# Hash products of the late head pairs ahead of the gated parts, q·k ahead of the bucket product, and another order of the first steps

## Chip, cores, metric

One core of a Trainium2 chip. The metric is device microseconds of one execution. Each comparison has its own runs of the kernel before on the same chip. A ratio is the mean time of one kernel's fast runs over that of the other's of the same rounds, so it is not quite the ratio of the medians quoted beside it.

## The reference, cut

```python
# attention, 4 batches x 8 heads x 768 x 64, 6 hash bits
q_bucket = sum((q @ proj > 0) * 2**i);  k_bucket = sum((k @ proj > 0) * 2**i)
scores = where(q_bucket == k_bucket, (q @ k.T) / 8, -1e9)
x = softmax(scores) @ v            # rearranged to 3072 x 512
# feed-forward
g = x @ w_gate;  out = (g * sigmoid(g) * (x @ w_val)) @ w_out
```

## The kernel before

Heads are worked in pairs, 16 pairs, numbered from 0 here ("pair 10" is the number). A pair has 12 score units (2 halves of queries x 6 chunks of keys), two to a step of the loop; I call these two scores a *duo* of scores, and the change from other matmuls to a duo a *turn*. A wait "in pair 10" is one for the signs of pair 10, while the scores of pair 9 run. A step issues in this order: two scores, the products with v of the step before, then parts ("atoms") of the feed-forward of the batch before, with pieces of the next pair's preparation between them. The schedule is manual: what is written first is first in each engine's order.

A *tile* is a buffer of the program; a *bank* is what its `bank` helper takes, 128 x 512 f32 of PSUM, and a score tile is declared as two of them. The late hash products land in such a tile, and *evictions* turn them into sign bits: the keys' on VectorE, the queries' on ScalarE. A *row* is one matmul record of the trace; an f32 product of one head is two rows (768 for 384 products), and the rows of the two heads run side by side (four take 0.81 us, at 486 ns each).

A score adds two products in PSUM: a bf16 product of sign bits, which is 0 for the same bucket and hugely negative otherwise, and the f32 product of q and k.

```python
sc_ps = tile_pool(name="sc_ps", bufs=2)      # tiles of two banks
mm_ps = tile_pool(name="mm_ps", bufs=3)      # tiles of one bank: parts of the feed-forward

def score(u):
    sc = score_tile("sc")
    for x, start in ((bits, True), (T, False)):          # bucket product, then q.k
        for h in range(2):
            nc.tensor.matmul(sc[:, h, 0:HQ], x["k", n][rows, ks], x["q", n][rows, qs], ...)
    nc.scalar.activation(ring[...], sc[:, :, 0:HQ], AF.Exp, scale=SCALE)

def hash_blocks():                            # pairs 8 to 15
    ps = front_bank("hps")                    # there: one bank of a two-bank score tile
    for i, (name, half) in enumerate(where):  # k0, k1, q0, q1: 32 rows each
        nc.tensor.matmul(ps[i*32 : (i+1)*32, 0:HQ], hash_w[name][:, 0:32], T[name, n][...])
    def evict(half, to):                      # keys' signs on VectorE, queries' on ScalarE
        ...
    return [four evictions, each of one key and one query block]

# the step
while atoms and credit >= atoms[0][0]:
    size, atom = atoms.pop(0)
    atom()                                    # a part: products, then its VectorE and ScalarE work
    while mine and size:                      # behind it: hash_blocks, later one eviction a part
        size -= 1
        mine[:1] = mine[0]() or []
```

The softmax here doesn't subtract the row's maximum and nothing guards it: scores larger than these inputs give would overflow.

Of the kernel before, what the change touches and what calls it, by code (L numbers as in the profile page):

```python
# [17 lines left out]
def kernel(  # L18
# [11 lines left out]
    nc = tc.nc  # L30
# [6 lines left out]
    HQ = CH * P  # L37
    BLOCK = 32
    NP = H // 2
# [30 lines left out]
    def bank(name):  # L70
        return mm_ps.tile([P, 512], FP32, tag="mm", name=name)

    def score_tile(name):
        return sc_ps.tile([P, 2, 512], FP32, tag="sc", name=name)
# [5 lines left out]
    def fetch(n, name, queue, half=None):  # L80
        b, pr = pairs[n]
        if name == "v":
            t = raws["v", n] = raw.tile([P, 2, NCH, D], FP32, tag="vraw", name="vraw")
            queue.dma_start(
                t.rearrange("p h c d -> p h (c d)"),
                v[b, 2 * pr : 2 * pr + 2].rearrange("h (p c) d -> p h (c d)", c=NCH),
            )
            return
        src = q if name == "q" else k
        if not half:  # L90
            raws[name, n] = raw.tile([P, NCH, 2, D], FP32, tag=name + "raw", name=name + "raw",
                                     bufs=1)
        t = raws[name, n]
        if n <= NP:
            cs = slice(None) if half is None else slice(half * CH, (half + 1) * CH)
            for h in range(2):
                queue.dma_start(t[:, cs, h, :],
                                src[b, 2 * pr + h].rearrange("(p c) d -> p c d", c=NCH)[:, cs, :])
            return


        blocks = t.rearrange("p c a b -> p (c a b)").rearrange(
            "p (c a d) -> p c a d", a=P // BLOCK, d=BLOCK)
        for h in range(2):
            for x in range(D // BLOCK):
                at = h * D + x * BLOCK
                queue.dma_start(
                    blocks[at : at + BLOCK],
                    src[b, 2 * pr + h][:, x * BLOCK : (x + 1) * BLOCK].rearrange(
                        "(a p c) d -> p c a d", c=NCH, p=BLOCK))  # L110

    def load(n):
        for name in "qkv":
            fetch(n, name, nc.sync)
# [20 lines left out]
    for _ in range(9):  # L135
        ps = bank("idle")
# [26 lines left out]
    hash_w = {}  # L163
# [36 lines left out]
    def load_words(i, queue=nc.gpsimd):  # L200
        if i < len(pieces):
            words[i] = wraw.tile([P, PIECE, 2], I32, tag="words", name="words")
            queue.dma_start(words[i].rearrange("p f w -> p (f w)"), pieces[i][1])
# [29 lines left out]
    def narrow_on(n):  # L233
        for _ in range(n):
            next(narrowing, None)

    load_words(0, nc.sync)
    load_words(1, nc.sync)
    load(1)


    T = {}
    bits = {}
    atoms = []

    def front_bank(name):

        if len(T) > 2 * 2 * NP:
            return score_tile(name)[:, 0, :]
        return bank(name)  # L250

    def front(n):


        def transpose(name, half):
            if (name, n) not in T:
                T[name, n] = opnd.tile([P, S], FP32, tag=name + "T", name=name + "T")
            ps = front_bank("tps")
            for i in range(CH):
                nc.tensor.transpose(ps[:, i * P : (i + 1) * P],  # L260
                                    raws[name, n][:, half * CH + i, :, :].rearrange("p h d -> p (h d)"),
                                    ident)
            nc.scalar.copy(T[name, n][:, half * HQ : (half + 1) * HQ], ps[:, 0:HQ])

        bits["q", n] = sides["q", n % 2]
        bits["k", n] = sides["k", n % 2]

        def sign(name, half, to, ps, at):
            o = bits[name, n][to, half * HQ : (half + 1) * HQ]
            if name == "q":  # L270
                nc.scalar.activation(o, ps[at, 0:HQ], AF.Sign, bias=nudge[to])  # L271
            else:
                nc.vector.tensor_scalar(o, ps[at, 0:HQ], scalar1=above_k[to], scalar2=times_k[to],  # L273
                                        op0=ALU.is_gt, op1=ALU.mult)

        def hash_bits(name, half):
            ps = front_bank("hps")
            nc.tensor.matmul(ps[:, 0:HQ], hash_w[name], T[name, n][:, half * HQ : (half + 1) * HQ],  # L278
                             start=True, stop=True)
            sign(name, half, slice(0, P), ps, slice(0, P))  # L280

        def hash_blocks():

            ps = front_bank("hps")
            where = [(name, half) for name in "kq" for half in range(2)]
            for i, (name, half) in enumerate(where):
                nc.tensor.matmul(ps[i * BLOCK : (i + 1) * BLOCK, 0:HQ], hash_w[name][:, 0:BLOCK],  # L287
                                 T[name, n][:, half * HQ : (half + 1) * HQ], start=True, stop=True)

            def evict(half, to):  # L290
                for i, x in enumerate(where):
                    if x[1] == half:
                        sign(x[0], half, slice(to, to + BLOCK), ps,
                             slice(i * BLOCK, (i + 1) * BLOCK))

            return [lambda half=half, to=to: evict(half, to) for half in range(2) for to in (0, D)]

        def transpose_blocks(name):
            T[name, n] = opnd.tile([P, S], FP32, tag=name + "T", name=name + "T")
            nc.vector.transpose(T[name, n], raws[name, n].rearrange("p c h d -> p (c h d)"))  # L300

        steps = []
        if n > NP:

            for name in "qk":
                steps.append(lambda name=name: transpose_blocks(name))
        if n >= 2 * NP:
            return steps + [hash_blocks]
        order = [("q", 0), ("k", 0), ("k", 1), ("q", 1)]
        for at in (order[0:2], order[2:3], order[3:4]) if n == 0 else (order,):  # L310
            if n <= NP:
                for x in at:
                    steps.append(lambda x=x: transpose(*x))
            for x in at:
                steps.append(lambda x=x: hash_bits(*x))
        return steps


    units = [(n, half, c) for n in range(len(pairs)) for half in range(2) for c in range(NCH)]
# [4 lines left out]
    def score(u):  # L324
        n, half, c = units[u]
        qs = slice(half * HQ, (half + 1) * HQ)
        ks = slice(c * P, (c + 1) * P)
        sc = score_tile("sc")
        for x, start in ((bits, True), (T, False)):
            for h in range(2):  # L330
                rows = slice(h * D, (h + 1) * D)
                nc.tensor.matmul(sc[:, h, 0:HQ], x["k", n][rows, ks], x["q", n][rows, qs],  # L332
                                 start=start, stop=not start)
        nc.scalar.activation(ring[u % RING][:, :, 0:HQ], sc[:, :, 0:HQ], AF.Exp, scale=SCALE)  # L334
# [214 lines left out]


    steps = front(0)
    for _ in range(4):
        steps.pop(0)()
    N = len(units)
    per = 2 * NCH
# [3 lines left out]
    for u in range(0, N + 2, 2):  # L559
        n, at = divmod(u, per)  # L560
        if u < N:
            if at == (4 if n == 0 else 0) and n + 1 < len(pairs):
                steps.extend(front(n + 1))
            if at == per - 2 and n + 2 < len(pairs):
                load(n + 2)
            score(u)
            score(u + 1)
        while due:
            norm(due.pop(0))
        for x in left:  # L570
            attend(x)
            if units[x][2] == NCH - 1:
                due.append(x)
        left = [u, u + 1]
        mine = [steps.pop(0) for _ in range(2) if (u < 4 or u % per >= 2) and steps]
        if not atoms:
            credit = 0.0
            while mine:
                mine[:1] = mine[0]() or []
            narrow_on(3 if u % 12 == 6 else 2)  # L580
            continue


        credit += 5.75 if n < 2 * NP else 5.5
        while atoms and credit >= atoms[0][0]:
            size, atom = atoms.pop(0)
            credit -= size
            atom()
            narrow_on(2 * size)
            while mine and size:  # L590
                size -= 1
                mine[:1] = mine[0]() or []
        while mine:
            mine[:1] = mine[0]() or []
# [36 lines left out]
```

## Time and profile before

| | kernel before |
|---|---|
| time, median of 4 runs | 1124.47 us (1123.0 to 1126.46) |
| span of the profiled run (a run of 1125.41 us, mean clock 0.991) | 1123.5 us |
| TensorE idle, sum of the gaps ahead of its instructions | 28.1 us |
| of this, scores that wait for hash evictions | 16.6 us, six waits |
| lost at half clock (half of TensorE's busy time there) | 8.1 us |

The last row is an estimate: TensorE was busy 16.3 us at a granted clock of 0.50, and half of that is 8.1. In one such stretch (557.6 to 560.8 us) a row of the products with v took 844 ns on average, against 495 between 489.3 and 553 us, at full clock. The prediction shows the lines behind these rows and how they are read. TensorE is busy 97% of the span.

### The profile page before, as it was taken

The numbers are of one execution on the slowest core, as the hardware profiler recorded it, in microseconds if no ns is written. First come the engines' busy times: TensorE is split into PE (matmuls) and PEld (weight loads), VectorE is DVE, ScalarE is ACT, GpSimd is POOL, SyncE is SP. The second block draws the span as 40 slices with busy tenths as digits, with TensorE's granted clock in tenths as the row PEclk, the third lists the DMA queues.
The fourth block names the chain that finished last, engine by engine and source line by source line (L and its number), as shares of the span: only waits on it lengthen the run. The fifth ranks groups of instructions, "written<-read, shape, count | busy, mean of one in ns | idle before, by whom it ended". The sixth has DMA issues, their size and how long they took to land.

```text
span 1123.5 us, 10819 instructions
## 1 busy us (share of the span) xinstructions
PE 1091.4 (97%) x4213; PEld 523.0 (47%) x4213; DVE 702.1 (62%) x1143; ACT 284.3 (25%) x449; POOL 21.0 (2%) x57
## 2 busy tenths in 40 slices
PE   8999999999999999989899999999989999999998
PEld 3444455454543445445444344544544444555543
DVE  4899989999863177766762327676766223677400
ACT  4545322222222222222222223222222120111100
POOL 1000000000000000000000000000000000000000
PEclk9999999999999999989999999998999999999999
DMA  5333422424201120200100212010000000000000
GB/s 141 90 95 66 104 78 83 108 88 101 85 31 40 40 38 1 43 0 15 29 1 24 47 33 38 15 29 1 15 0 1 19 10 28 1 1 0 1 29 28
DMA packets 97843, 44.74 MB, mean 40 GB/s; under 512 B 86016, under 2 KB 90112, under 8 KB 97792
## 3 DMA queue, kind: packets, MB, share of 16 engines
q1 hardware_dynamic: 92032, 26.03, 10.2%
q0 software_dynamic: 4960, 17.83, 5.1%
q8 instruction: 33, 0.54, 0.2%
q10 hardware_dynamic: 800, 0.20, 0.1%
q14 instruction: 18, 0.15, 0.0%
HBM read 37.75 MB, written 6.29 MB: 39 GB/s over the span
## 4 chain that ended last, share of the span: by engine, by line
PE 85%; DVE 9%; ACT 3%; issue 1%; DMA 0%; POOL 0%; SPq 0%; DVEq 0%; ACTq 0%; POOLq 0%
PE up L455 27%; PE po L531 22%; PE sc L332 11%; PE av L343 11%; PE up L401 9%; PE sum L364 2%; ACT A L334 2%; PE hps L278 1%; DVE kb L273 1%; DVE r L367 1%; DVE acc L351 1%; ACT qb L271 1%; DVE c L383 1%; PE tps L260 1%; PE hps L287 1%
## 5 line engine op out<-in xcount | busy, mean ns | idle before, releaser
L531 PE MATMUL po<-wo,ht 128*128 128x512 f32 x576 | 255.2, 597 | 0.0
L334 ACT ACTIVATE A<-sc 128x768 f32<-128x768 f32 x192 | 153.9, 811 | 221.7 <-PE sc L332 199.6
L367 DVE RECIPROCAL r<-sum 128x384 f32<-128x384 f32 x32 | 81.8, 2556 | 150.0 <-PE sum L364 149.9
L531 PEld LDWEIGHTS po<-wo,ht 128*128 128x128 f32 x576 | 107.1, 190 | 140.6 <-issue 139.6
L332 PE MATMUL sc<-qT,kT 64*128 64x384 f32 x768 | 156.6, 486 | 0.0
L343 PE MATMUL av<-A,vraw 128*64 128x386 f32 x768 | 149.0, 510 | 0.0
L351 DVE TENSOR_TENSOR acc<-acc,A 128x768 f32<-128x768 f32 x128 | 122.2, 955 | 24.6 <-ACT A L334 19.6
L455 PE MATMUL up<-xT,ws 128*128 128x384 f32 x288 | 106.1, 491 | 0.0
L343 PEld LDWEIGHTS av<-A,vraw 128*64 128x64 f32 x768 | 50.3, 139 | 84.0 <-issue 83.6
L332 PE MATMUL sc<-qb,kb 64*128 64x384 bf16 x384 | 64.0, 330 | 17.4 <-ACT qb L271 16.6
L467 DVE TENSOR_TENSOR c<-c,up 128x384 f32<-128x384 f32 x108 | 57.5, 549 | 35.8 <-PE up L455 35.7
L332 PEld LDWEIGHTS sc<-qT,kT 64*128 64x128 f32 x768 | 69.3, 190 | 19.6 <-issue 19.6
L467 DVE TENSOR_TENSOR ht<-ht,up 128x384 f32<-128x384 f32 x108 | 57.3, 550 | 30.8 <-PE up L455 29.8
L455 PEld LDWEIGHTS up<-xT,ws 128*128 128x128 f32 x288 | 53.9, 191 | 43.3 <-issue 4.8
L401 PE MATMUL up<-xT,wv 128*128 128x384 f32 x192 | 67.3, 492 | 0.5 <-DVE wv L226 0.3
L401 PE MATMUL up<-xT,wg 128*128 128x384 f32 x192 | 66.9, 491 | 0.5 <-DVE ht L386 0.5
L382 ACT ACTIVATE c<-up 128x384 f32<-128x384 f32 x42 | 20.6, 490 | 164.2 <-PE up L401 103.6
L332 PEld LDWEIGHTS <-kb 64*128 64x128 bf16 x384 | 19.3, 93 | 88.1 <-issue 73.7
L273 DVE TENSOR_SCALAR kb<-hps,columns 32x384 bf16<-32x384 f32 (+1 forms) x48 | 32.1, 669 | 35.2 <-PE hps L287 22.6
L535 ACT COPY o<-po 128x512 f32<-128x512 f32 x24 | 14.0, 585 | 158.0 <-PE po L531 158.0
L455 PE MATMUL up<-xT,wg 128*128 128x384 f32 x144 | 54.0, 498 | 0.0
L455 PE MATMUL up<-xc,ws 128*128 128x384 f32 x144 | 52.9, 490 | 1.0 <-DVE c L467 1.0
(99 smaller groups left out, 987.4 us busy)
## 6 DMA issues: line engine op xcount, KB each, us to landing
vraw<-in_v_dram SPq DMA_DIRECT2D x16, 384.0 KB, 3.2
words<-in_moe_w_val_dram POOLq DMA_DIRECT2D x12, 512.0 KB, 3.8
words<-in_moe_w_out_dram POOLq DMA_DIRECT2D x12, 512.0 KB, 3.5
out_dram<-o SPq DMA_DIRECT2D x24, 256.0 KB, 2.0
words<-in_moe_w_gate_dram POOLq DMA_DIRECT2D x10, 512.0 KB, 3.9
qraw<-in_q_dram SPq DMA_DIRECT2D x48, 96.0 KB, 3.3
kraw<-in_k_dram SPq DMA_DIRECT2D x46, 96.0 KB, 3.3
qraw<-in_q_dram SPq DMA_DIRECT2D x8, 192.0 KB, 3.4
```

The source lines that it names most:

```text
L273: nc.vector.tensor_scalar(o, ps[at, 0:HQ], scalar1=above_k[to], scalar2=times_k[to], op0=ALU.is_gt, op1=ALU.mult)
L332: nc.tensor.matmul(sc[:, h, 0:HQ], x["k", n][rows, ks], x["q", n][rows, qs], start=start, stop=not start)
L334: nc.scalar.activation(ring[u % RING][:, :, 0:HQ], sc[:, :, 0:HQ], AF.Exp, scale=SCALE)
L343: nc.tensor.matmul(ps[h * D : (h + 1) * D, 0:AW], raws["v", n][:, h, c, :], a[:, h, :], start=c == 0, stop=c == NCH - 1)
L351: nc.vector.tensor_tensor(acc[n, half], acc[n, half], a[:, :, 0:HQ], op=ALU.add)
L364: nc.tensor.matmul(ps[h * D : (h + 1) * D, 0:HQ], ones, t[:, h, :], start=True, stop=True)
L367: nc.vector.reciprocal(r, ps[:, 0:HQ])
L382: nc.scalar.activation(th, g, AF.Tanh, scale=0.5)
L401: nc.tensor.matmul(ps, w[:, j, f * P : (f + 1) * P], x[j][:, halves[half]], start=j == 0, stop=j == NJ - 1)
L455: nc.tensor.matmul(ps, a[:, j], xs[j], start=start and j == 0, stop=j == 1, skip_group_check=True)
L467: nc.vector.tensor_tensor(out_, a, b, op=op)
L531: nc.tensor.matmul(ps, hs[f, half][:, i * P : (i + 1) * P], wo[:, f, :], start=f == 0, stop=f == NF - 1)
```

## The change

Its intent is to take the six waits and the idle start away: hash products earlier in their step, so that their evictions end earlier; keys and queries in different banks, in the hope that VectorE and ScalarE don't hold each other up then (31 waits of ScalarE for VectorE, 44.8 us, in the kernel before); q·k ahead of the bucket product, so that signs come later to be needed; and first steps in an order that needs no copy at once.

```diff
-    load(1)
+    for name, queue in (("q", nc.sync), ("k", nc.gpsimd), ("v", nc.sync)):
+        fetch(1, name, queue)
...
         def hash_blocks():
-            ps = front_bank("hps")
+            tile_ = score_tile("hps")
             for i, (name, half) in enumerate(where):
-                nc.tensor.matmul(ps[i * BLOCK : (i + 1) * BLOCK, 0:HQ], ...
+                parts[name, half] = ps = tile_[i * BLOCK : (i + 1) * BLOCK, i // 2, :]
+                nc.tensor.matmul(ps[:, 0:HQ], ...
...
-        for at in (order[0:2], order[2:3], order[3:4]) if n == 0 else (order,):
-            ...
+        if n == 0:
+            return turns[0:3] + hashes[0:2] + [hashes[2], turns[3], hashes[3]]
...
-        for x, start in ((bits, True), (T, False)):
+        for x, start in ((T, True), (bits, False)):
...
-    for _ in range(4):
+    for _ in range(5):
         steps.pop(0)()
...
         credit += 5.75 if n < 2 * NP else 5.5
+        if len(mine) == 1 and n + 1 >= 2 * NP:
+            mine = mine[0]()
         while atoms and credit >= atoms[0][0]:
```

More of the change, by code (lines that the diff above doesn't have):

```diff
@@ L246, in front_bank @@
     def front_bank(name):
-        if len(T) > 2 * 2 * NP:
-            return score_tile(name)[:, 0, :]
         return bank(name)
@@ L282, in hash_blocks @@
         def hash_blocks():
-            ps = front_bank("hps")
+            tile_ = score_tile("hps")
             where = [(name, half) for name in "kq" for half in range(2)]
+            parts = {}
             for i, (name, half) in enumerate(where):
-                nc.tensor.matmul(ps[i * BLOCK : (i + 1) * BLOCK, 0:HQ], hash_w[name][:, 0:BLOCK],
+                parts[name, half] = ps = tile_[i * BLOCK : (i + 1) * BLOCK, i // 2, :]
+                nc.tensor.matmul(ps[:, 0:HQ], hash_w[name][:, 0:BLOCK],
                                  T[name, n][:, half * HQ : (half + 1) * HQ], start=True, stop=True)
             def evict(half, to):
-                for i, x in enumerate(where):
-                    if x[1] == half:
-                        sign(x[0], half, slice(to, to + BLOCK), ps,
-                             slice(i * BLOCK, (i + 1) * BLOCK))
+                for name in "kq":
+                    sign(name, half, slice(to, to + BLOCK), parts[name, half], slice(0, BLOCK))
             return [lambda half=half, to=to: evict(half, to) for half in range(2) for to in (0, D)]
@@ L309, in front @@
         order = [("q", 0), ("k", 0), ("k", 1), ("q", 1)]
-        for at in (order[0:2], order[2:3], order[3:4]) if n == 0 else (order,):
-            if n <= NP:
-                for x in at:
-                    steps.append(lambda x=x: transpose(*x))
-            for x in at:
-                steps.append(lambda x=x: hash_bits(*x))
-        return steps
+        turns = [lambda x=x: transpose(*x) for x in order] if n <= NP else []
+        hashes = [lambda x=x: hash_bits(*x) for x in order]
+        if n == 0:
+            return turns[0:3] + hashes[0:2] + [hashes[2], turns[3], hashes[3]]
+        return steps + turns + hashes
     units = [(n, half, c) for n in range(len(pairs)) for half in range(2) for c in range(NCH)]
```

## The prediction

> **What bounds the kernel now.** I read the page first: the summary of engines, the clock row, the chain of work that ended last. Then who waited for whom on TensorE alone, and last the timelines around each wait.
>
> ```profile
> span 1123.5 us, 10819 instructions
> PE 1091.4 (97%) x4213; PEld 523.0 (47%) x4213; DVE 702.1 (62%) x1143; ACT 284.3 (25%) x449; POOL 21.0 (2%) x57
> PEclk9999999999999999989999999998999999999999
> PE 85%; DVE 9%; ACT 3%; issue 1%; DMA 0%; POOL 0%; SPq 0%; DVEq 0%; ACTq 0%; POOLq 0%
> ```
>
> TensorE is busy 97% of the span and every stage runs at its pace. The matmuls themselves are not changed in number or size (the diff only moves them), so what can be won is TensorE's idle time, 1123.5 - 1091.4 = 32 us, and the few places where its clock falls. The view of TensorE's waits says what the idle time is:
>
> ```profile
> PE sc L332 <- ACT qb L271: 16.6, 6, 4.3
> PE tps L260 <- DMA kraw<-in_k_dram: 1.4, 1, 1.4
> PE hps L278 <- ACT kT L263: 0.8, 1, 0.8
> PE sc L332 <- DVE kb L273: 0.8, 1, 0.8
> PE hps L278 <- ACT qT L263: 0.6, 1, 0.6
> ```
>
> The first line is half of it: six waits, 16.6 us. From the timelines they begin before 347.79, 484.70, 556.44, 624.48, 760.75 and 832.70 us and last 0.45, 4.33, 3.15, 1.64, 3.88 and 3.15 us. All six are one thing: the late head pairs (from the ninth) put their four hash products into a two-bank score tile; the pool has two such tiles, so the second score after it needs that tile back, and it comes back only when all four sign evictions of keys (VectorE) and queries (ScalarE) are through. Head pairs 9 and 13 show no wait. The other four lines, 3.6 us, are all in the first 23 us.
>
> The long waits cost twice. Table of stretches (window, busy time of PE, PEld, DVE, ACT, POOL, then the clock):
>
> ```profile
> 482.38:489.21 6.83, 4.50 (x15) 1.42 (x14) 3.49 (x5) 2.77 (x4) 0.00 (x0) 0.50 0.00 0
> 557.48:560.89 3.41, 3.41 (x10) 1.12 (x11) 1.81 (x5) 1.28 (x2) 0.00 (x0) 0.50 0.00 0
> 622.32:625.73 3.41, 1.77 (x12) 0.66 (x10) 2.70 (x4) 2.13 (x4) 0.00 (x0) 1.00 0.00 0
> 758.86:765.69 6.83, 4.94 (x15) 1.86 (x15) 3.08 (x4) 3.06 (x5) 0.00 (x0) 0.50 0.00 0
> 833.96:837.37 3.41, 3.41 (x10) 1.32 (x7) 1.16 (x4) 1.05 (x2) 0.00 (x0) 0.50 0.00 0
> ```
>
> After the four waits over 3 us the clock is 0.50. TensorE was busy 4.50 + 3.41 + 4.94 + 3.41 = 16.3 us at half speed, so 8.1 us were lost on top of the 16.6. The 1.64 us wait left the clock at 1.00.
>
> What VectorE does while TensorE waits, here in the wait that ends at 556.44 (timeline of VectorE):
>
> ```profile
> 550.77 0.55 DVE L386 SCALAR_TENSOR_TENSOR ht<-c,ht 128x384 f32<-128x384 f32 x1
> 551.36 0.67 DVE L273 TENSOR_SCALAR kb<-hps,columns 32x384 bf16<-32x384 f32 x1
> 552.06 0.56 DVE L467 TENSOR_TENSOR ht<-ht,up 128x384 f32<-128x384 f32 x1
> 552.65 0.56 DVE L386 SCALAR_TENSOR_TENSOR ht<-c,ht 128x384 f32<-128x384 f32 x1
> 553.24 0.67 DVE L273 TENSOR_SCALAR kb<-hps,columns 32x384 bf16<-32x384 f32 x1
> 553.94 0.55 DVE L467 TENSOR_TENSOR ht<-ht,up 128x384 f32<-128x384 f32 x1
> 554.52 0.56 DVE L386 SCALAR_TENSOR_TENSOR ht<-c,ht 128x384 f32<-128x384 f32 x1
> 555.11 0.67 DVE L273 TENSOR_SCALAR kb<-hps,columns 32x384 bf16<-32x384 f32 x1
> ```
>
> It runs back to back: the fourth key eviction is late because it stands behind the gated work of all five feed-forward parts. ScalarE's last query eviction follows at 555.82. The wait is named after ScalarE, but VectorE's order makes it.
>
> [...] ScalarE's qb waits for VectorE's kb 31 times, 44.8 us. [...] the stretch ahead of 482.38 had 2.01 us idle from 480.37 on and tripped, 1.64 us did not. [...] SyncE issues keys at 17.52, behind the queries whose buffer comes free at 16.1.
>
> **Part 1: hash ahead of the gated parts, banks apart.** The four products come before the step's first part, and each eviction follows one part earlier, so the fourth stands behind four parts and not five. With keys and queries in their own banks I take the alternation to go away; ScalarE then has its evictions done early and the fourth key eviction sets the end.
>
> Pair 11 (wait to 556.44): the four hash products take 0.77 us of TensorE (546.17 to 546.95) and go ahead, so only the first part moves, to 545.45; its VectorE work starts 1.60 later (as now: 546.95 to 548.54), at 547.05, the first eviction at 547.65. Part two is ready at 548.54 as before, second eviction 549.02; part three 549.83, third eviction 551.36; part four 552.06 and 552.65, fourth 553.24 to 553.91. These are today's starts, one eviction further. The score could start at 553.29 (556.44 - 3.15) and starts at about 553.95: 0.66 in place of 3.15. Pair 15 has the same timeline: again 0.66.
>
> Pairs 10 and 14 have gates, where VectorE also waits for ScalarE's tanh: add to gate op 1.20, gate op to eviction 0.48, eviction to next add 0.62, sum 2.3 a part. Pair 10: part one moves 0.77 to 474.13, its eviction at 475.77; add 476.40, second eviction 478.08; add 478.70, third 480.40; then four weight sums, 0.46 + 0.46 + 0.34 + 0.45 after a 0.70 eviction, fourth 482.81 to 483.48. The score could start at 480.37: 3.16 in place of 4.33. Pair 14 has three weight sums and the same steps: released at 759.5, wanted at 756.87: 2.66 in place of 3.88.
>
> Pairs 8 and 12 stand among down products, with VectorE free: evictions are done before the score asks (ScalarE at about 622.2 against 622.7 in pair 12). 0.45 and 1.64 go to 0.
>
> Left: 3.16 + 2.66 + 0.66 + 0.66 = 7.1 of 16.6 us; **gained 9.5**. Clock: 0.66 trips nothing. [...] 2.4 us stay of 8.1; **gained 5.7**.
>
> **Part 2: start.** The third transpose goes ahead of the first hash; its keys land at about 5.9, so the first hash moves from 6.03 to 6.4 (-0.37). The transpose (0.40) is gone later, and so are the waits for copies (0.81 and 0.57), as copies lie a step ahead. Product of q and k first puts 0.65 us of f32 matmul into the wait for the first key signs (0.77). The second query transpose comes at about 10.5 rather than 15.54, so queries of pair 1 are fetched 5 us earlier, and keys by GpSimd no longer queue behind them: 1.42 gone. **Gained 0.40 + 0.81 + 0.57 + 0.65 + 1.42 - 0.37 = 3.5.**
>
> **Part 3: q·k first elsewhere.** Nowhere after 13.2 us does a score wait for bits as data, so this gains nothing there. It might cost at the turn from other matmuls: the f32 weights take 190 ns to load, the bf16 ones 93. But av to the bf16 score takes 1.45 us now (38.73 to 40.18), av to an f32 hash 1.44 (34.08 to 35.52), so the load's length doesn't show: 0.
>
> Sum 9.5 + 5.7 + 3.5 = 18.7: 1125.6 - 18.7 = **1107**.
>
> **Rivals.** (a) The alternation between the banks is the whole cause, and the waits vanish: 16.6 + 8.1 + 3.5 = 28 us, 1097. For it: every qb waits for a kb. Against: VectorE's line is dense in four of six waits, and it is in order. (b) The evictions keep a mutual wait, or VectorE falls further behind because the first part is 0.77 later: the four long waits shrink by well under 1 us each, the clock still falls; with the start some 8 us, 1117. For it: pairs 10 and 14 gain only a part's work. (c) The f32 load shows at each of 96 turns, 0.09 us each: 9 us given back, 1116. Against: the equal turns above.
>
> **Range and chances.** The trips alone swing 2.4 us down and 3 up; VectorE's chain in pairs 10 and 14 is good to half a microsecond each; the turn of part 3 to 1.5 us in all. Range 1100 to 1113. Faster by over 2% means under 1103.5, nearer to rival (a): 0.2. Slower needs something not seen in this profile: 0.01.
>
> **What would show it.** Right: TensorE's waits of scores for hash evictions fall to about 7 us, named after VectorE's kb, in two waits of near 3 us and two under 1; one or two stretches at 0.50; no qb waiting for kb in the late pairs; the first av product near 12.5 us (14.09 now) and no wait for keys by 23. Wrong: no wait at all (a); waits over 3 us still in all four places (b); pair of scores over 1.72 us (c).

## The result and the profile after

1118.51 us (median of 4, 1117.8 to 1120.9) against 1124.47: ratio 0.995, 95% interval 0.9926 to 0.9974. All outputs are right. Faster by half a percent, clear of noise, but a third of what was predicted and outside its range of 1100 to 1113. Lines of the page after (the score's lines are L330 there and L332 before, its evictions L270 and L272, before L271 and L273; the parts' products L453, before L455; in the runs below lines shift by one to three again):

```profile
span 1117.0 us, 10825 instructions
...
PE 1095.1 (98%) x4213; PEld 526.1 (47%) x4213; DVE 701.7 (63%) x1143; ACT 285.0 (26%) x449; POOL 22.7 (2%) x59
...
PEclk9999999999999999989999999999999999999999
```

TensorE's busy time did not fall with the span but rose, 1091.4 to 1095.1 us, with the same 4213 matmuls and less time at half clock. That is the first sign that instructions are spaced wider. TensorE's waits after (who waited for whom: total us, times, longest):

```profile
PE sc L330 <- ACT qb L270: 11.6, 6, 3.9
...
PE sum L362 <- ACT A L332: 1.1, 2, 0.5
...
PE tps L259 <- DMA kraw<-in_k_dram: 0.2, 1, 0.2
```

The start is cleared (1.4, 0.8, 0.8, 0.6 us of waits became 0.2), but the waits for evictions fell only to 11.6 us and are still named after ScalarE. And in the table of stretches the half clock is still there, 5.82 + 3.41 us of busy time, so 4.6 us lost by the same estimate:

```profile
482.50:489.32 6.82, 5.82 (x16) 2.26 (x17) 2.72 (x4) 2.68 (x4) 0.00 (x0) 0.50 0.00 0
758.98:762.39 3.41, 3.41 (x10) 1.18 (x7) 0.57 (x1) 1.20 (x2) 0.00 (x0) 0.50 0.00 0
```

I then laid the start of every duo of scores after against the same one before. By the fourth duo, at 23 us, the change is ahead by 4.20 us. From there on it loses 0.09 us a duo, steadily (85 to 98 ns in most duos), but for half a microsecond won in pair 8; ahead of the wait in pair 10 it is only 0.79 us in front, and it wins again where waits shrink (3.4 us in each of two pairs). The timeline of TensorE around one turn from hash products to scores, before:

```profile
36.27 0.81 PE L278 MATMUL hps<-qT,hashq 128*128 128x384 f32 x2
37.01 0.34 PE L332 MATMUL sc<-qb,kb 64*128 64x384 bf16 x2
37.19 0.81 PE L332 MATMUL sc<-qT,kT 64*128 64x384 f32 x4
37.83 0.33 PE L332 MATMUL sc<-qb,kb 64*128 64x384 bf16 x2
```

and the same place after:

```profile
32.37 0.81 PE L277 MATMUL hps<-qT,hashq 128*128 128x384 f32 x2
33.10 0.92 PE L330 MATMUL sc<-qT,kT 64*128 64x384 f32 x4
33.85 0.33 PE L330 MATMUL sc<-qb,kb 64*128 64x384 bf16 x2
34.02 0.81 PE L330 MATMUL sc<-qT,kT 64*128 64x384 f32 x4
34.66 0.33 PE L330 MATMUL sc<-qb,kb 64*128 64x384 bf16 x2
```

The first four f32 rows after the turn take 0.75 us to the next instruction (33.10 to 33.85), the second four 0.64 (34.02 to 34.66). Before, the bf16 rows at the turn took 0.18 (37.01 to 37.19) and the f32 rows 0.64. From the first row of a duo to what follows it the median is 1.719 us before and 1.816 after: 0.097 us more; 96 times that is 9.3 us. The group's mean shows it too, 486 ns before (first line) and 512 after:

```profile
L332 PE MATMUL sc<-qT,kT 64*128 64x384 f32 x768 | 156.6, 486 | 0.0
```

```profile
L330 PE MATMUL sc<-qT,kT 64*128 64x384 f32 x768 | 166.8, 512 | 11.6 <-ACT qb L270 11.6
```

The busy time of the group, in which rows that run side by side count once, rose by as much: from 156.6 to 166.8 us.

### The profile page after: what moved, and what is told of

The parts are those of the page before. It is cut to its first block, busy times and chain, and to the rows that moved or that the text cites. A ratio compares the mean times of both kernels' runs of the same rounds, so it can differ in the third digit from the quotient of the medians.

```text
span 1117.0 us, 10825 instructions
## 1 busy us (share of the span) xinstructions
PE 1095.1 (98%) x4213; PEld 526.1 (47%) x4213; DVE 701.7 (63%) x1143; ACT 285.0 (26%) x449; POOL 22.7 (2%) x59
## 4 chain that ended last, share of the span: by engine, by line
PE 90%; DVE 5%; ACT 3%; issue 1%; DMA 0%; SPq 0%; ACTq 0%; DVEq 0%
PE up L453 26%; PE po L529 22%; PE sc L330 13%; PE av L341 12%; PE up L399 10%; PE sum L362 2%; PE hps L277 2%; ACT A L332 2%; DVE kb L272 1%; ACT qb L270 1%; DVE c L381 1%; PE tps L259 1%; ACT th L380 1%; PE hps L289 1%; DVE r L365 0%
## 5 line engine op out<-in xcount | busy, mean ns | idle before, releaser
L332 ACT ACTIVATE A<-sc 128x768 f32<-128x768 f32 x192 | 154.1, 811 | 225.6 <-PE sc L330 203.9
L330 PE MATMUL sc<-qT,kT 64*128 64x384 f32 x768 | 166.8, 512 | 11.6 <-ACT qb L270 11.6
L341 PE MATMUL av<-A,vraw 128*64 128x386 f32 x768 | 146.6, 503 | 0.0
L453 PE MATMUL up<-xT,ws 128*128 128x384 f32 x288 | 106.7, 493 | 0.0
L330 PEld LDWEIGHTS sc<-qT,kT 64*128 64x128 f32 x768 | 62.9, 186 | 88.9 <-issue 61.0
L453 PEld LDWEIGHTS up<-xT,ws 128*128 128x128 f32 x288 | 54.5, 192 | 43.0 <-issue 5.6
L399 PE MATMUL up<-xT,wv 128*128 128x384 f32 x192 | 67.3, 492 | 0.3 <-DVE wv L226 0.3
L399 PE MATMUL up<-xT,wg 128*128 128x384 f32 x192 | 66.9, 491 | 0.4 <-DVE ht L384 0.4
L330 PE MATMUL sc<-qb,kb 64*128 64x384 bf16 x384 | 63.4, 324 | 0.0
L453 PE MATMUL up<-xc,ws 128*128 128x384 f32 x144 | 52.9, 490 | 1.0 <-DVE c L465 1.0
L272 DVE TENSOR_SCALAR kb<-hps,columns 32x384 bf16<-32x384 f32 (+1 forms) x48 | 32.1, 669 | 33.6 <-ACT qb L270 15.9
L453 PE MATMUL up<-xc,wg 128*128 128x384 f32 x144 | 53.2, 492 | 0.0
L453 PE MATMUL up<-xT,wv 128*128 128x384 f32 x144 | 52.9, 490 | 0.0
```

What stands on the lines that cost most here:

```text
L272: nc.vector.tensor_scalar(o, ps[at, 0:HQ], scalar1=above_k[to], scalar2=times_k[to], op0=ALU.is_gt, op1=ALU.mult)
L332: nc.scalar.activation(ring[u % RING][:, :, 0:HQ], sc[:, :, 0:HQ], AF.Exp, scale=SCALE)
L341: nc.tensor.matmul(ps[h * D : (h + 1) * D, 0:AW], raws["v", n][:, h, c, :], a[:, h, :], start=c == 0, stop=c == NCH - 1)
L399: nc.tensor.matmul(ps, w[:, j, f * P : (f + 1) * P], x[j][:, halves[half]], start=j == 0, stop=j == NJ - 1)
L453: nc.tensor.matmul(ps, a[:, j], xs[j], start=start and j == 0, stop=j == 1, skip_group_check=True)
```

## The experiments

Theories at the outset. **Theory 1**: the loss is the f32 weight load at each turn into a duo of scores (rival (c) of the prediction), and the rest of the change works. **Theory 2**: the order within a score is free, and the loss comes from the hash products ahead of the parts. For the waits that stayed, **theory A**: the engines' mutual waits follow the tile, not the bank; **theory B**: something else, the bank or the data, makes them alternate.

### One part undone, one part alone

**e1_bits_first**: the change, with the old order within a score.

```diff
-        for x, start in ((T, True), (bits, False)):
+        for x, start in ((bits, True), (T, False)):
```

> The change with one thing undone: the bucket product stands ahead of q times k again in every score. Theory 1 (the f32 weight load shows at the turn into each of the 96 pairs of scores, 1.816 us a pair after the change against 1.719 before): the pair goes back to about 1.72 us, and the kernel gets faster than the change by 96 x 0.097 = 9.3 us, less 0.65 us that the first score loses again and about 2 us where the wait of the row sum for ScalarE (0.157 us, hidden by the longer pair) comes back: about 1111 us. Theory 2 (the lost microseconds are due to the hash ahead of the parts, and the order within a score is free): no faster than the change, 1118 us, and the pair stays at 1.816.

Measured: 1111.56 us (1110.94 to 1111.96) against 1124.66 before, ratio 0.9883; median duo 1.719 us; waits for evictions 12.2 us. Theory 1 as expected, theory 2 falls: undoing one line of the change makes it 7 us faster.

```profile
L330 PE MATMUL sc<-qT,kT 64*128 64x384 f32 x768 | 155.9, 484 | 0.0
```

**e2_qk_first_only**: the kernel before with only that line.

```diff
-        for x, start in ((bits, True), (T, False)):
+        for x, start in ((T, True), (bits, False)):
```

> The kernel before with one thing done: q times k ahead of the bucket product. Theory 1: every pair of scores takes 1.816 us, the waits on the last evictions stay at some 16.6 us, so the kernel is slower than before by 7 to 9 us: about 1132 us. Theory 2: same as before within 1 us, pair 1.72.

Measured: 1132.86 us (1132.68 to 1133.49) against 1124.66, ratio 1.0074; median duo 1.816 us. So this part alone costs 8.2 us net (7.3 between the two profiled runs). The net is less than 9.3 because TensorE's idle time falls too, from 28.1 to 25.4 us: the first score's wait for key signs (0.8) is filled, the waits for evictions fall from 16.6 to 16.1, and the idle time ahead of the row sums from 4.2 to 3.5. (e1 allowed about 2 us for the row sums; they still wait, 0.144 us where it was 0.157.)

**e3_start_only**: the kernel before with the new queue and the new order of first steps.

> The kernel before with the other order of first steps and the other queue for the keys of the second head pair, nothing else. Both theories: the first score of the third pair of scores comes earlier and nothing after 23 us changes: 3.5 to 4.5 us faster than before (the trace of the change shows 4.2 at 23 us, of which the order within the first score is 0.65 less 0.39 for four turns).

Measured: 1120.69 us (1120.27 to 1121.38), 4.0 us faster, ratio 0.9965. The time is as expected, but not all of it is the start: laid against the kernel before, e3 is 3.25 us ahead at 23 us and still 3.2 at 479. The rest comes later, where the half clock falls differently: with the same six waits (16.6 us) it covered 6.16 + 3.42 + 3.42 us of busy time, so 6.5 us were lost, not 8.1 (mean granted clock of the profiled runs 0.994, 0.991 before).

**e4_late_only**: the kernel before with the hash products ahead and in two banks of one tile; bucket product first, old start.

> The kernel before with only the late part: hash products ahead of the step's parts, keys and queries in two banks of one tile; bucket product first, old start. Theory 1: waits of scores for the last evictions fall from 16.6 to about 12 us, the clock loss from 8.1 to about 4.6, so 6 to 10 us faster than before: about 1116 us. Theory 2: the late part is what costs, no faster than before.

Measured: 1115.7 us (1115.36 to 1116.02), 9.0 us faster, ratio 0.992; waits for evictions 12.2 us. The half clock covered 3.42 + 5.60 us of busy time: 4.5 us lost. As theory 1 has it. The three parts sum to -4.0 - 9.0 + 8.2 = -4.8 us; the whole change measured -6.0. The 1.2 us between are not resolved: the clock's stretches fall differently in each run.

### Where the order within a score costs

**e5_qk_first_second**: the change, with q·k first only in the second score of each duo and in the very first score.

```diff
-        for x, start in ((T, True), (bits, False)):
+        for x, start in ((T, True), (bits, False)) if u % 2 or u == 0 else ((bits, True), (T, False)):
```

> The change with q times k first only in the second score of each pair (and in the very first score); the first score of a pair, the one behind other matmuls, has the bucket product first. Theory 1 (the f32 load shows only at the turn from other matmuls): pair 1.72 us, and the kernel is as fast as with the bucket product first everywhere, less 0.65 us at the start: about 1111 us. Rival (q times k ahead of the bucket product costs in every score, for another reason): half of the 0.097 us a pair stays, 1.77 us a pair, about 1115 us.

Measured: 1112.41 us (1110.4 to 1113.48) against 1124.21, ratio 0.9891; median duo 1.719 us. The time scatters more than the expected gain over e1, but the duo decides: q·k first is free behind another score and costs 0.097 us behind other matmuls. So it is the turn, not the order as such.

What differs at the turn is the load: the f32 keys take 182 to 190 ns to load, the bf16 ones 93, and the difference of the two (187 - 93 = 94 ns) is as large as the cost (97). Lines of the page before:

```profile
L332 PEld LDWEIGHTS sc<-qT,kT 64*128 64x128 f32 x768 | 69.3, 190 | 19.6 <-issue 19.6
...
L332 PEld LDWEIGHTS <-kb 64*128 64x128 bf16 x384 | 19.3, 93 | 88.1 <-issue 73.7
```

At the turn the first load begins together with its own matmul (18.886 and 18.887 us in the change); inside a duo it runs beside the matmuls of the score before (from 19.64 us for f32 rows at 19.80, beside bf16 rows that run from 19.64 on).

The kept trace of the kernel before shows more. I compared its turns behind the start, of all products, where no wait and no half clock disturbs them. Where the form of the product changes (the 128\*128, 128\*64, 128\*32 or 64\*128 of the lines), the first load begins with its own matmul (within 3 ns in the median), and the row behind it comes late, here by more the longer the load is: 10 ns for the bf16 keys (load 93 ns), 24 for the late hash products (106), 51 for the products with v (133), 104 for f32 parts (186). Each is the load less about 82 ns. At the 31 turns from row sums to products with v the form stays (both 128\*64), and nothing is lost: the load runs one row ahead (it begins at 221.153 us for a matmul at 221.473) and the next row is on time (0.324 us). So in this trace the cost goes with the load's length at a change of form. What makes it so, no run shows.

### Whether the banks count

**e6_banks_only**: the kernel before with keys and queries in two banks of the one tile, hash products and evictions where they were.

```diff
-            ps = front_bank("hps")
+            tile_ = score_tile("hps")
...
-                nc.tensor.matmul(ps[i * BLOCK : (i + 1) * BLOCK, 0:HQ], ...
+                parts[name, half] = ps = tile_[i * BLOCK : (i + 1) * BLOCK, i // 2, :]
...
```

> The kernel before with keys and queries of the late hash products in two banks of the one tile, nothing else. Theory A (the mutual waits of the two engines follow the tile, not the bank): scores wait 16.6 us as before, the queries' evictions still wait for the keys' ones, 1124 to 1125 us. Theory B (the bank is what counts): the queries' evictions no longer wait, the six waits shrink by about 0.6 us each and the one at 624 us vanishes, about 4 us faster.

Measured: 1123.9 us against 1124.21, ratio 0.9999. The hash tile's view: who waited for it, and how often VectorE's evictions kept ScalarE idle (us, times):

```profile
  DVE kb L271: 44.8, 31
...
  PE sc L331: 17.4, 7
```

These are the numbers of the kernel before, to the digit:

```profile
  DVE kb L273: 44.8, 31
...
  PE sc L332: 17.4, 7
```

Theory A: separate banks within one tile buy nothing here.

**e7_two_tiles**: as e5, with queries in one score tile and keys in the next.

```diff
-            tile_ = score_tile("hps")
+            tiles = {name: score_tile("hps") for name in "qk"}
...
-                parts[name, half] = ps = tile_[i * BLOCK : (i + 1) * BLOCK, i // 2, :]
+                parts[name, half] = ps = tiles[name][i * BLOCK : (i + 1) * BLOCK, 0, :]
```

> As the run before the last (q times k first in the second score only), and the late hash products in two tiles, queries in the first, keys in the second, so that the second score behind them waits for keys alone. Theory A (mutual waits follow the tile): no query eviction waits for a key eviction in the late head pairs, the waits of scores fall from 11.6 us to about 7 (3.2, 2.7, 0.6, 0.6, none at the down products) and are named after the keys' evictions; about 1105 us. Theory B (something else makes them alternate): waits 11.6 us, 1111 us.

Measured: 1107.24 us (1102.34 to 1108.93) against 1124.21, ratio 0.9836. TensorE's waits:

```profile
PE sc L330 <- ACT qb L270: 4.9, 2, 2.5
...
PE sc L330 <- DVE kb L272: 2.6, 4, 0.9
```

No query eviction waits for a key eviction in the late pairs any more, and the sum is 7.5 us as theory A said. But two thirds of it are named after ScalarE: in the pairs with gates the query evictions stand behind ScalarE's tanh, which wait for VectorE in turn (54 waits, 86.5 us, in the whole run). My expectation had ScalarE early; it is not. The order of the evictions behind the parts holds both engines. And the half clock did not shrink: it covered 6.22 + 3.10 us of busy time, 4.7 us lost, as in the change (mean granted clock 0.995 in both).

### The place of the evictions

**e8_all_evictions**: as e7, with all four evictions directly behind the hash products, ahead of the first part.

```diff
         if len(mine) == 1 and n + 1 >= 2 * NP:
-            mine = mine[0]()
+            for step in mine.pop()():
+                step()
```

> The two tiles, and all four evictions issued directly behind the hash products, ahead of the first gated part. If what is left of the waits is VectorE's order (evictions behind gated parts), they vanish, the clock stays at full, and the time falls to some 1097 us. Rival: the gated parts, 2.7 us later on VectorE, then hold the matmuls' banks, and a wait of an up product for VectorE of 1 to 3 us a head pair takes their place: 1100 to 1108 us.

Measured: **1095.08 us** (1094.71 to 1095.21) against 1124.21, ratio 0.9738 (0.9723 to 0.9753). No score waits for an eviction, and the mean granted clock is 1.0, in all four runs; of the rival's waits one came, 0.4 us. The gain over e7, 12.2 us, is what the waits (7.5) and the half clock (4.7) had cost there. The timeline of pair 10's hash products and evictions in this run:

```profile
466.91 1.56 PE L453 MATMUL up<-xc,wg 128*128 128x384 f32 x4
467.01 2.72 DVE L272 TENSOR_SCALAR kb<-hps,columns 32x384 bf16<-32x384 f32 x4 [0.59 <-PE hps L289]
467.07 2.33 ACT L270 ACTIVATE qb<-hps,columns 32x384 bf16<-32x384 f32 x4 [1.41 <-PE hps L289]
...
469.76 1.02 DVE L465 TENSOR_TENSOR c<-c,up 128x384 f32<-128x384 f32 x2
```

Both engines work side by side and are done 2.8 us after the hash products, and the first part's adds are only 1.3 us later than their product (about 468.5: 466.91 and the usual 1.60). This version beats both kernels: 2.6% faster than before, and 23 us under the change's median.

**e9_first_one_tile**: as e8, in the one tile of the change.

> As the fastest run so far (all evictions directly behind the hash products, ahead of the first gated part), but with keys and queries in the one two-bank tile of the change. If the place of the evictions in VectorE's order is what made the scores wait, the waits stay gone although the two engines alternate again (four pairs of 0.67 + 0.58 and two hand-overs, about 5.3 us behind the hash products, while the tile is wanted some 7.4 us behind them): 1095 to 1099 us, with up to 1 us a head pair in new waits of up products for VectorE. If the two tiles were the cause of the gain: near 1105 us or more.

Measured: 1104.87 us (1104.07 to 1106.1) against 1125.37, ratio 0.9822. A miss: I allowed up to 1 us a pair in new waits, and six new ones came to 8.8 us, 0.6 to 2.3 each, on the banks of the feed-forward parts:

```profile
PE up L453 <- DVE c L465: 4.5, 4, 1.7
PE up L453 <- DVE ht L465: 4.2, 2, 2.3
...
PE up L453 <- ACT o L533: 1.2, 2, 0.6
```

(Of the first line's four waits two, 3.4 us, are new; the other two, 0.5 us each, are in every run.) The scores' waits did vanish, and the mean granted clock was 1.0 in the profiled run. But alternating in one tile, the evictions hold VectorE for 4.6 us (468.39 to 473.02 in pair 10, against 2.7), the parts' sums come later, and the parts' three banks come free too late. So the two tiles are worth some 9 to 10 us (1104.87 against 1095.08, on two chips; ratios 0.9822 and 0.9738) once the evictions stand together.

**e10_before_at_once**: the kernel before with the four evictions issued together, behind the first part and in one bank.

```diff
-            return [lambda half=half, to=to: evict(half, to) for half in range(2) for to in (0, D)]
+            for half in range(2):
+                for to in (0, D):
+                    evict(half, to)
```

> The kernel before with one thing changed: the four pairs of evictions are issued all at once behind the hash products, where these stand already (behind the first part), in one bank. If VectorE's order is the cause, most of the 16.6 us of waits and of the 8.1 us of half clock go: the tile is free about 5.3 us behind the hash products at 473.9, 479.3, where the score wants it at 480.4, so about 1100 us. If the alternation in one bank is the cause, the waits stay above 10 us: 1115 us or more.

Measured: 1114.6 us (1114.32 to 1115.41) against 1125.37, ratio 0.991. The waits of scores fell from 16.6 to 1.6 us, so the place in the order made them; but waits of up products took over most of it, some 10 us that the kernel before does not have:

```profile
PE up L457 <- DVE c L469: 5.1, 4, 2.0
PE up L457 <- ACT c L490: 3.5, 2, 1.8
PE up L457 <- DVE ht L388: 2.5, 2, 1.3
...
PE sc L334 <- ACT qb L271: 1.6, 1, 1.6
```

So neither expectation held in full: the time is near the 1115 us of the one, and the waits of scores went as the other said. The wait moved to another pool of banks.

## Why the prediction was wrong, point by point

- **The bound and the two costs of a wait: right.** From before over the change to e8 the half clock goes with the long waits (8.1, 4.6 and 0 us lost), though not in each run (see the clock below), and e8 gained all three: waits, clock, start.
- **Part 3, "the load's length doesn't show: 0": this step failed.** It is the largest error: predicted +0.65 us of gain with the first score's share, measured alone 8.2 us of loss. The equal turns I compared, 1.45 and 1.44 us, ran from the first av product to the *start* of the next matmul. There the first row was no later for its load of 190 ns than for one of 93; what came late was the row *after* it. The profile before had it: the hash products, the f32 matmuls whose turn I used as evidence, have a longest row of 590 ns against a median of 486, and the row behind the first one comes 0.43 us later (35.52, 35.95), the next one 0.32 (36.27). Rival (c) had the size right (0.09 us a turn), and its sign, a duo over 1.72 us, came (1.816); it was dismissed by that reading. Its 1116 us is close partly by luck, since it left the late part's shortfall out.
- **Part 1, "I take the alternation to go away": failed.** VectorE's order was worked out well: in pair 11 the fourth key eviction was to come at 553.24, and it came at 553.02 with the kernel 0.11 us ahead. But the alternation stayed: both banks are one tile. The assumption behind it, that the waits follow the bank, does not hold: with two banks the same 31 waits stayed (e6), with two tiles none (e7). With the alternation, each wait ends with ScalarE's last eviction, about 0.6 us behind VectorE's. In pair 12 it is worse: the second key eviction waits for the first query eviction, and that stands in ScalarE's order behind an output copy that waits for TensorE. The timeline after:

```profile
613.17 0.67 DVE L272 TENSOR_SCALAR kb<-hps,columns 32x384 bf16<-32x384 f32 x1 [5.53 <-PE hps L289]
...
615.96 0.59 ACT L533 COPY o<-po 128x512 f32<-128x512 f32 x1 [4.17 <-PE po L529]
616.57 0.57 ACT L270 ACTIVATE qb<-hps,columns 32x384 bf16<-32x384 f32 x1
...
617.18 0.67 DVE L272 TENSOR_SCALAR kb<-hps,columns 32x384 bf16<-32x384 f32 x1 [3.34 <-ACT qb L270]
```

  VectorE sits 3.34 us with nothing else to do. Predicted 0 there, measured 1.67 us. In all 7.1 us of waits were predicted and 12.2 measured in the late part alone (11.6 in the change, where the longer first score of a duo hides 0.1 of each).
- **Clock: the half clock at the long waits came again, the predicted size was too small, and the same waits don't always cost the same.** 2.4 us were to stay, by an estimate of mine that no run shows; 4.6 stayed. The two waits in the pairs with gates are 3.9 and 3.5 us long and not 3.2 and 2.7; at both the granted clock was 0.50 for a stretch, of 6.82 and 3.41 us, which cost 2.9 and 1.7 us. When the clock falls is not explained here: in the kernel before it fell 2.01 and 1.99 us into two of the waits over 3 us, and 1.0 and 1.3 us behind the end of the two others; the wait of 1.64 us left it at 1.00. What these waits cost in clock was not fixed: with the six waits of the kernel before, 8.1 us were lost in its profile, 6.5 in e3, 6.3 in e6; and e7 lost 4.7 us with no wait over 2.5, while its fastest run (1102.34 us) had a mean clock of 1.0. So differences of up to 1.8 us between these runs can come from this alone (8.1 less 6.3).
- **Part 2, the start: right.** 2.85 us without the first score's order; measured 4.0 in e3, of which 3.25 at 23 us. The third transpose did not push the first hash back as far as feared (6.24 and not 6.4).
- **The sum.** Of 18.7 us: part 3 is off by 8.9 (0.65 + 8.2), the late part by 6.2 (15.2 predicted, 9.0 measured), the start by 1.1 the other way (0.4 of it in the start itself). That leaves 4.7; measured were 6.0. The forecast started from 1125.6 us, the median of the three runs known then, and 2% under that is 1103.1, not 1103.5.
- **Rival (b)** had the late part's outcome partly right (waits over 3 us stayed in two of four places, 0.4 us shorter each; the other two shrank by 2.0). Its 1117 us is nearest to the result, but by luck: the late part alone gained 9.0 us (e4), and the order within a score took 8.2 back (e2). Rival (a), that the alternation is the whole cause, is wrong: without it (e7) 7.5 us of waits stay. Nor is the order the whole cause: without the alternation the evictions together gain 12 us (e7 to e8), with it they leave 8.8 us of new waits (e9).

## What to carry to other kernels

Of an order swap that "adds nothing", ask what the first instruction behind a change of shape must load (here f32 keys, 182 to 190 ns, or bf16 ones, 93: 0.097 us a turn between them), and measure the turn to the second row behind it, not the first. Evictions that free a buffer did best here all together, ahead of the parts whose work they had stood behind, with a tile for each engine (e8); in one shared tile the same order made 8.8 us of new waits (e9). Handing them out one a part tied the buffer to the slowest part's chain (scores waited 16.6 us for it in the kernel before, 7.5 in e7). And see whether the program's waits follow the tile or the bank before splitting banks: two tiles gave what two banks in a tile did not (no wait of a query eviction for a key eviction in e7 and e8, 31 in e6, 44.8 us).
